# Loading the first head pair in halves, and a new written-out order, in a sparse-attention plus ELU-MLP kernel

## The chip, the cores and the metric

The kernel runs on one core of a Trainium2 chip. The metric is the device time of one execution in microseconds (us); lower is better. The program is bound to one core, so nothing is shared with another core by the program itself.

## The reference

```python
# q, k, v: (8, 8, 576, 64)  (batch, heads, positions, head size)
scores = q @ k.transpose(0, 1, 3, 2) / sqrt(64)
rel = pos[:, None] - pos[None, :]
mask_local   = (rel >= 0) & (rel < 32)                 # heads 0 to 3
mask_strided = (rel >= 0) & (pos % 32 equal for both)  # heads 4 to 7
attn = softmax(where(mask, scores, -1e9))
x = (attn @ v).transpose(0, 2, 1, 3).reshape(8 * 576, 8 * 64)   # 4608 tokens x 512
h = x @ w_in                                            # 512 -> 2048
g = where(h > 0, h, exp(min(h, 0)) - 1)                 # ELU
out = g @ w_out                                         # 2048 -> 512, float32
```

## The kernel before

All data is cast to bf16 on the way in; sums are kept in float32 in PSUM, whose eight banks of 512 columns are one tile `ps` that the program hands out by hand.

**Attention.** A sequence of 576 positions is cut into 8 residues of 72 rows each (for the strided heads, key and query of one residue meet only within it) or into six blocks of 96 (for the local heads). The heads of a batch come in four pairs: two strided (`s0`, `s1`) and two local (`l0`, `l1`), and each pair in two halves `u`. For batches 0 and 1 the rows of q and k are brought into columns by TensorE transposes (`transposes`, then `copy_T` out of PSUM); for later batches a DMA does it (`dma_T`). A pair then goes through `scores` (TensorE), `exp_s` (ScalarE), `mask` (VectorE), `pv` (TensorE: values and, for the softmax's sum, a matmul with ones), `log_sums` and `recip` (ScalarE: logarithm, and exponential of its negative), and `write_x` (VectorE), which puts the result into `xT`, the transposed input of the MLP.

**MLP.** The 4608 tokens are nine chunks of 512. The first product of a chunk is 16 steps of four matmuls over 512 columns (`l1`; in chunk 0 its four parts are split in two, first the two that need the strided heads alone, then the two that need the local heads). ELU is `exp_h` (ScalarE), `clamp` (VectorE or ScalarE) and `elu` (VectorE). The second product (`l2`) is four groups of 16 matmuls, then a copy out of PSUM and a store.

**Order.** Nothing is left to a scheduler: the string `ORDER` names every step, and each engine and each DMA queue takes its steps in that order. A token is a letter and its arguments: `T` transposes, `C`/`c` `copy_T` on ScalarE/VectorE, `S` scores, `e` exponential, `m` mask, `O` values, `n` logarithm, `r` reciprocal, `x` write to `xT`; `a`, `b` the two halves of a first-product step of chunk 0, `L` a whole one, `h`, `i`/`j`, `g` the ELU; `Z` a quarter of a second-product group, `o`/`q` its copy, `t` its store, `Y`/`y` the last group in pieces; `D` a load (`load`), `F` a fill of masks or ones, `V`, `W` copies of v, `X` a transposing DMA, `k`/`K` a cast of the staged q and k. In `S`, `O`, `T`, `a`, `L`, `Z` the last figures are PSUM banks. `w` is a run of matmuls on a tile of zeros (`warm`), whose result nobody reads; it fills TensorE's time in the first 20 us.

**The start.** q and k of the first strided pair (heads 4 and 5 of batch 0) are loaded ahead of the order by `load_stage`, each as one float32 transfer from SyncE's queue into `stage`, and cast by `cast`, one head at a time on ScalarE and VectorE. Everything else is loaded, and cast on the way, from GpSimd's queue, in the order of the `D` tokens: the second strided pair's q and k (`load_runs` of two heads), then v of the strided heads, k and q of the local heads, v of the local heads, and the weights in pieces of 512 columns (`wi1` holds steps 4 to 7 of the first product, `wi0` 0 to 3, `wi2` 8 to 11, `wi3` 12 to 15). One `load_runs` is a single transfer of all four heads.

Of the kernel before, what the change touches and what calls it, by code (L numbers as in the profile page):

```python
# [9 lines left out]
BF16 = mybir.dt.bfloat16  # L10
# [6 lines left out]
D = 64  # L17
# [28 lines left out]
i.0.7 a.0.11.7 g.0.1 h.0.3 b.0.0 g.0.7 h.0.5 T.1s1.q.1 b.0.6 h.0.0 i.0.2 a.0.8.3 c.1s1.q h.0.6 b.0.11  # L46
g.0.2 j.0.0 D.vs.1 a.0.13.1 i.0.3 b.0.8 h.0.11 g.0.0 a.0.12.5 j.0.5 g.0.3 b.0.13 i.0.6 a.0.14.0 h.0.13
b.0.12 g.0.6 D.vl.1 a.0.10.2 g.0.5 h.0.12 a.0.9.4 h.0.8 i.0.12 b.0.10 j.0.11 b.0.14 j.0.13 Z.0.0.0.6
g.0.11 h.0.10 D.vs.2 g.0.13 Z.0.2.0.7 h.0.14 g.0.12 j.0.14 Z.0.1.0.1 i.0.8 D.ks.2 i.0.10 Z.0.2.1.7
g.0.10 g.0.14 b.0.9 D.qs.2 T.1s0.q.5 g.0.8 h.0.9 T.1s1.k.2 a.0.15.0 c.1s0.q j.0.9 Z.0.1.1.1 c.1s1.k  # L50
# [20 lines left out]
L.2.2.6 W.3 h.2.7 i.2.7 L.2.11.5 D.vs.4 h.2.2 g.2.7 D.vl.3 L.2.3.4 h.2.11 j.2.2 i.2.11 S.3s0.0.01
S.3s0.1.23 L.2.6.7 g.2.2 e.3s0.0 D.qs.4 g.2.11 h.2.3 L.2.5.6 D.ks.4 e.3s0.1 m.3s0.0 i.2.3 h.2.6 D.ql.4
L.2.9.5 m.3s0.1 h.2.5 i.2.6 L.2.0.3 g.2.3 h.2.9 g.2.6 j.2.9 L.2.10.4 i.2.5 h.2.0 g.2.9 O.3s0.1.01 h.2.10
L.2.4.7 g.2.5 j.2.10 i.2.0 L.2.8.5 h.2.4 g.2.10 n.3s0.1 L.2.14.6 i.2.4 D.kl.4 g.2.0 h.2.8 L.2.1.4 g.2.4
# [638 lines left out]
```

## Time and profile before

| | us |
|---|---|
| median of 3 runs (lowest, highest) | 309.84 (309.32, 311.02) |
| the profiled execution, its own time | 310.17 |
| its span from first to last instruction | 308.5 |
| TensorE, busy | 300.1 (97% of the span) |
| ScalarE, busy | 231.1 (75%) |
| VectorE, busy | 224.9 (73%) |
| GpSimd, busy | 78.9 (26%) |

Instructions are named by the line of the kernel that issues them: L376 is a matmul on zeros, L382 a cast of staged q or k, L394 and L397 TensorE's transposes (strided, local), L405 to L409 the copies out of PSUM, L433 the scores, L440 their exponential, L447 and L453 the masks, L460 to L481 the values of batches 0 and 1 and their sums, L531 the logarithm, L536 the reciprocal, L561 the write to `xT`, L588 the first product, L622 the second, L596 to L616 the ELU. L231, L254, L265 and L269 are GpSimd's loads. The page counts a matmul as busy to its modelled end, which lies beyond the start of the next, so a busy TensorE does not say that no slot between two starts was lost.

### The profile page before, as it was taken

To read this page: it belongs to the slowest core of one execution; us is meant where nothing else is said; L and a number is where in the kernel's file an instruction comes from. 1 tells how busy PE (TensorE), PEld (TensorE's weight loads), DVE (VectorE), ACT (ScalarE), POOL (GpSimd) and SP (SyncE) were. 2 spreads that over 40 slices of the span, in tenths; PEclk is the share of its full clock that TensorE was granted. 3 is DMA by queue.
4 is the path that set the end of the run, shared out by engine and by line. 5 is a ranking of instruction groups with operands and counts; after the bars stand their busy time and mean duration, and the time that the engine had idled before them with its cause. 6 is when DMAs were issued, how large, how long until landed. Compare 5 with 4: busy or idle time off the path is not lost.

```text
span 308.5 us, 6465 instructions
## 1 busy us (share of the span) xinstructions
PE 300.1 (97%) x2452; PEld 154.0 (50%) x2452; DVE 224.9 (73%) x432; ACT 231.1 (75%) x413; POOL 78.9 (26%) x107
## 2 busy tenths in 40 slices
PE   8999999999999999999999999999999999999992
PEld 8864455445544454444544555454444544444452
DVE  6667969699679977996779879976688548984010
ACT  4888768689969898996998988888786577872120
POOL 8823345171029108530861250000000000000000
PEclk9999999999999999999999999999999999999999
DMA  8999999999909999999999199504110030100152
GB/s 165 192 208 205 207 194 176 144 216 156 203 9 167 160 225 116 163 187 158 193 187 125 17 145 189 108 24 130 56 34 0 2 102 0 36 1 0 36 162 77
DMA packets 106879, 37.61 MB, mean 122 GB/s; under 512 B 89024, under 2 KB 102048, under 8 KB 106848
## 3 DMA queue, kind: packets, MB, share of 16 engines
q0 software_dynamic: 69600, 19.43, 61.2%
q1 hardware_dynamic: 37088, 17.70, 30.3%
q8 instruction: 19, 0.31, 0.4%
q14 instruction: 12, 0.10, 0.1%
q10 hardware_dynamic: 160, 0.07, 0.1%
HBM read 39.47 MB, written 9.44 MB: 159 GB/s over the span
## 4 chain that ended last, share of the span: by engine, by line
PE 86%; DVE 4%; ACT 3%; DMA 3%; issue 1%; POOL 1%; POOLq 0%; DVEq 0%; ACTq 0%
PE ps L622 39%; PE ps L588 35%; PE ps L433 3%; DMA ql<-in_q_dram 3%; PE ps L503 2%; PE ps L496 2%; ACT he L596 1%; PE ps L652 1%; PE ps L376 1%; DVE he L605 1%; ACT he L603 1%; DVE g L616 1%; DVE g L614 1%; ACT e L440 1%; PE ps L397 1%
## 5 line engine op out<-in xcount | busy, mean ns | idle before, releaser
L622 PE MATMUL ps<-w_out_sb,g 128*128 128x512 bf16 x560 | 133.4, 379 | 0.3 <-DVE g L614 0.3
L588 PE MATMUL ps<-xT,w_in_sb 128*128 128x512 bf16 x576 | 132.4, 379 | 0.8 <-DVE g L616 0.4
L596 ACT ACTIVATE he<-ps 128x512 f32<-128x512 f32 x144 | 80.4, 595 | 27.8 <-PE ps L588 25.9
L588 PEld LDWEIGHTS <-w_in_sb 128*128 128x128 bf16 x576 | 54.5, 98 | 64.7 <-issue 2.8
L622 PEld LDWEIGHTS <-g 128*128 128x128 bf16 x560 | 51.1, 98 | 55.2 <-issue 0.4
L616 DVE TENSOR_TENSOR g<-he,ps 128x512 bf16<-128x512 bf16 x90 | 60.0, 681 | 1.7
L561 DVE TENSOR_TENSOR xT<-ps,ln 64x576 bf16<-64x576 f32 (+1 forms) x64 | 42.6, 677 | 18.3 <-ACT ln L536 17.8
L440 ACT ACTIVATE e<-ps 72x576 bf16<-72x576 f32 (+1 forms) x64 | 39.1, 646 | 10.8 <-PE ps L433 9.2
L614 DVE SCALAR_TENSOR_TENSOR g<-he,ps 128x512 bf16<-128x512 bf16 x54 | 36.4, 681 | 14.2 <-ACT he L603 14.0
L605 DVE TENSOR_SCALAR he<-he 128x512 bf16<-128x512 f32 x90 | 39.0, 442 | 8.2 <-ACT he L596 7.4
L531 ACT ACTIVATE ln<-ps 64x576 f32<-64x576 f32 (+1 forms) x64 | 36.3, 583 | 8.9 <-PE ps L503 3.8
L536 ACT ACTIVATE ln<-ln 64x576 f32<-64x576 f32 (+1 forms) x64 | 38.9, 621 | 1.4
L603 ACT ACTIVATE he<-he 128x512 bf16<-128x512 f32 x54 | 33.4, 628 | 1.3 <-DVE g L616 0.7
L628 DVE COPY osb<-ps 128x512 f32<-128x512 f32 x23 | 15.7, 685 | 11.6 <-PE ps L622 11.1
L244 POOL DMA_DIRECT2D kl<-in_k_dram x24 | 17.7, 744 | 21.9 <-DMA kTl<-kl 9.5
L237 POOL DMA_DIRECT2D ql<-in_q_dram x24 | 19.6, 822 | 7.7 <-DMA w_out_sb<-in_moe_w_out_dram 4.3
L453 DVE TENSOR_TENSOR pm<-e,mask_l 128x576 bf16<-128x576 bf16 x32 | 14.3, 456 | 7.6 <-ACT e L440 7.0
L447 DVE TENSOR_TENSOR pm<-e,mask_s 72x576 bf16<-72x576 bf16 x32 | 14.2, 447 | 4.6 <-ACT e L440 4.4
L628 ACT COPY osb<-ps 128x512 f32<-128x512 f32 x12 | 7.0, 586 | 13.5 <-PE ps L622 13.5
L376 PE MATMUL ps<-zero 128*128 128x128 bf16 x148 | 12.7, 251 | 1.4 <-DVE zero L293 1.1
L231 POOL DMA_DIRECT2D vs<-in_v_dram x7 | 4.7, 669 | 35.2 <-DVE he L605 18.5
L254 POOL DMA_DIRECT2D vl<-in_v_dram x8 | 9.7, 1213 | 15.6 <-PE ps L503 12.4
(87 smaller groups left out, 160.7 us busy)
## 6 DMA issues: line engine op xcount, KB each, us to landing
out_dram<-osb SPq DMA_DIRECT2D x32, 144.0 KB
vl<-in_v_dram POOLq DMA_DIRECT2D x8, 288.0 KB, 8.4
w_in_sb<-in_moe_w_in_dram POOLq DMA_DIRECT2D x4, 512.0 KB, 13.5
w_out_sb<-in_moe_w_out_dram POOLq DMA_DIRECT2D x4, 512.0 KB, 17.6
vs<-in_v_dram POOLq DMA_DIRECT2D x6, 320.0 KB, 7.0
ql<-in_q_dram POOLq DMA_DIRECT2D x24, 72.0 KB, 8.2
kl<-in_k_dram POOLq DMA_DIRECT2D x24, 72.0 KB, 7.7
ks<-in_k_dram POOLq DMA_DIRECT2D x5, 320.0 KB, 7.9
```

Of the source, the lines that this page charges most:

```text
L440: nc.scalar.activation(e[0:R], tiles.pop(("S", key, u))[0:R], ACT.Exp, scale=scale)
L531: nc.scalar.activation(t, s_ps, ACT.Ln)
L536: nc.scalar.activation(t, t, ACT.Exp, scale=-1.0)
L561: nc.vector.tensor_mul(dst, o_ps, rc)
L588: nc.tensor.matmul(tiles["h", ch, m], lhsT=w_in_sb[:, c, m * 128:(m + 1) * 128], rhs=xT[:, c, ch * CHUNK:(ch + 1) * CHUNK], start=(c == 2) ...
L596: nc.scalar.activation(e, tiles["h", i[0], i[1]], ACT.Exp)
L603: nc.scalar.activation(e1, e, ACT.Relu, bias=1.0, scale=-1.0)
L605: eng.tensor_scalar(e1, e, scalar1=1.0, scalar2=1.0, op0=ALU.min, op1=ALU.subtract)
L614: nc.vector.scalar_tensor_tensor(dst, e1, -1.0, h, op0=ALU.mult, op1=ALU.max)
L616: nc.vector.tensor_tensor(dst, e1, h, op=ALU.max)
L622: nc.tensor.matmul(ops, lhsT=g[ch % 2][:, m, kk * 128:(kk + 1) * 128], rhs=w_out_sb[:, m, :], start=(m == 0), stop=(m == MC - 1), skip_gro ...
L628: eng(o_sb, tiles.pop(("o", int(ch), int(kk))))
```

## The change

`load_stage` is gone. q and k of the first pair are each loaded in two halves of every run, 256 of its 512 elements each, as four transfers: q's two from SyncE's queue and k's two from ScalarE's queue, ahead of the activation table. `cast` takes a half of both heads instead of one head. `transposes` and `copy_T` take an optional part, and for the first pair do four of the eight blocks at a time. `load` takes an optional pair `y`, so that the order can load two heads of four; v of the strided heads and q and k of the local heads of batch 0 are loaded so, as six transfers in place of three. The tile of zeros has 512 columns instead of 128, and `warm` takes a list of widths. The whole of `ORDER` is new: the order of steps in all nine chunks, the banks, and which engine takes some of the copies and clamps. The computation is the same.

```diff
 ORDER = """
-w.7.46 D.vs.0 F.vp D.kl.0 F.v1 D.ql.0 k.q.1 K.q.0 D.vl.0 F.ms T.0s0.q.7 D.wi1.0 k.k.0 K.k.1 D.wi0.0
-C.0s0.q w.3.26 T.0s0.k.6 T.0s1.k.5 C.0s0.k D.wi2.0 C.0s1.k D.qs.1 w.3.12 S.0s0.0.67 T.0s1.q.4 e.0s0.0
-S.0s0.1.01 c.0s1.q e.0s0.1 w.5.7 S.0s1.0.23 D.wi3.0 S.0s1.1.45 m.0s0.1 m.0s0.0 F.mk e.0s1.1 w.3.12
...
-D.kl.1 m.0l0.0 w.7.11 a.0.5.6 r.0l1.1 m.0l0.1 a.0.7.3 n.0l1.0 x.0l1.1 O.0l0.1.21 r.0l1.0 O.0l0.0.05
-n.0l0.1 x.0l1.0 a.0.6.4 n.0l0.0 a.0.4.7 r.0l0.1 r.0l0.0 D.wo2.0 a.0.2.5 x.0l0.1 x.0l0.0 a.0.1.1 a.0.3.2
-b.0.7 b.0.4 h.0.7 b.0.1 h.0.4 D.ql.1 b.0.2 h.0.1 b.0.5 i.0.4 a.0.0.0 g.0.4 j.0.1 b.0.3 D.wo3.0 h.0.2
...
+w.7.512.512.512.512.512.512.512.512 D.ql.0.1 F.vp D.kl.0.1 F.v1 D.ql.0.0 k.q.0 F.ms D.vs.0.0 T.0s0.q.0.7
+D.kl.0.0 K.q.1 K.k.1 D.vs.0.1 K.k.0 C.0s0.q.0 w.0.512.512.512.512.512 T.0s0.k.0.6 D.vl.0 T.0s0.k.1.5
+T.0s0.q.1.4 c.0s0.k.0 T.0s1.k.7 c.0s0.k.1 c.0s1.k w.0.324 T.0s1.q.6 c.0s0.q.1 D.wi1.0 S.0s0.0.01 c.0s1.q
+S.0s0.1.23 e.0s0.0 w.5.185 S.0s1.0.45 D.qs.1 S.0s1.1.67 e.0s1.0 m.0s0.0 w.2.224.224 T.0l1.k.1 D.wi3.0
+e.0s1.1 m.0s1.0 w.0.499 T.0l0.q.0 C.0l1.k D.wi0.0 m.0s1.1 T.0l1.q.7 e.0s0.1 c.0l1.q w.4.155 O.0s0.0.16
+D.wi2.0 c.0l0.q n.0s0.0 w.4.314 S.0l1.1.45 S.0l1.0.23 m.0s0.1 F.mk r.0s0.0 T.0l0.k.7 O.0s0.1.60 e.0l1.1
+x.0s0.0 D.wo0.0 F.ml e.0l1.0 w.0.224.224.102 O.0s1.1.15 c.0l0.k n.0s0.1 D.wo1.0 w.4.247 O.0s1.0.43
+n.0s1.1 m.0l1.0 n.0s1.0 r.0s1.1 D.ql.1 w.2.512.512.108 S.0l0.0.23 x.0s1.1 e.0l0.0 V.0 w.7.512.331
+S.0l0.1.01 r.0s1.0 m.0l1.1 r.0s0.1 w.7.512 O.0l1.0.75 m.0l0.0 e.0l0.1 O.0l1.1.32 x.0s1.0 n.0l1.0 m.0l0.1
+w.2.224.224 O.0l0.0.10 n.0l1.1 x.0s0.1 r.0l1.0 w.1.142 O.0l0.1.54 r.0l1.1 x.0l1.0 D.ks.1 n.0l0.0
+w.4.224.224 a.0.5.6 x.0l1.1 n.0l0.1 a.0.7.7 r.0l0.0 a.0.4.0 r.0l0.1 x.0l0.0 a.0.6.4 D.kl.1 x.0l0.1
+T.1s1.q.3 b.0.5 c.1s1.q b.0.7 h.0.5 b.0.4 h.0.7 i.0.5 b.0.6 h.0.4 g.0.5 T.1s0.q.5 D.wo2.0 a.0.12.3
+C.1s0.q i.0.4 a.0.13.6 h.0.6 g.0.4 a.0.14.5 b.0.12 a.0.15.2 h.0.12 b.0.15 j.0.6 D.vs.1 a.0.2.1 j.0.12
+b.0.13 g.0.6 b.0.2 h.0.13 g.0.12 a.0.1.4 h.0.2 i.0.7 b.0.1 i.0.13 a.0.3.3 g.0.7 h.0.1 D.wo3.0 b.0.3
+i.0.2 b.0.14 h.0.3 g.0.2 a.0.0.7 j.0.1 b.0.0 a.0.11.1 g.0.1 h.0.0 a.0.10.0 h.0.14 D.vl.1 i.0.0 b.0.10
...
-    zero = consts.tile([128, 128], BF16, tag="zero", name="zero")
+    zero = consts.tile([128, CHUNK], BF16, tag="zero", name="zero")
...
-    def load(what, b):
+    def load(what, b, y=None):
         nm, b = what[:2], int(b)
+        if y is not None:
+            load_runs(nm, b, 2 * int(y), 2)
+            return
...
-    load_stage(0, q)
-    load_stage(1, k)
+    def half(t, i):
+        return t.rearrange("p (h f) -> p h f", h=2)[:, :, i * NS * D // 2:(i + 1) * NS * D // 2]
+
+    for eng, n, x in ((nc.sync, 0, q), (nc.scalar, 1, k)):
+        for i in range(2):
+            rows, in_ = runs(x, 0, HG, 2)
+            f = NS * D // 2
+            eng.dma_start(out=half(stage[0:rows, n * 4 * f:(n + 1) * 4 * f], i),
+                          in_=in_[:, :, i * f:(i + 1) * f])
     nc.scalar.preload_act_table_set("natural_log_exp_and_others")
     load_runs("qs", 0, 2, 2)
     load_runs("ks", 0, 2, 2)
...
-    def warm(bank, n):
-        for _ in range(int(n)):
-            nc.tensor.matmul(ps[:, int(bank), 384:512], lhsT=zero, rhs=zero, start=True, stop=True,
+    def warm(bank, *cols):
+        for n in cols:
+            nc.tensor.matmul(ps[:, int(bank), CHUNK - int(n):], lhsT=zero[:, 0:128], rhs=zero[:, 0:int(n)],
+                             start=True, stop=True, skip_group_check=True)
...
+    def cast(eng, nm, i):
+        n, f = "qk".index(nm), 2 * NS * D
+        eng(half(raw[nm + "s"][0:RS, 0:f], int(i)), half(stage[0:RS, n * f:(n + 1) * f], int(i)))
```

More of the change, by code (lines that the diff above doesn't have):

```diff
@@ L46 @@
[L46 to L50, printed above, removed]
@@ L71 @@
[L71 to L74, printed above, removed]
-h.2.14 i.2.8 r.3s0.1 O.3s0.0.23 i.2.14 L.2.12.7 g.2.8 n.3s0.0 X.qs.4 g.2.14 r.3s0.0 L.2.13.5 x.3s0.1
@@ L372, in local_cols, with transposes @@
         return t.rearrange("k (s b p) -> k b s p", s=NS, b=3)[:, i]
[L374 to L389 removed]
+    def warm(bank, *cols):
[5 more added lines that the diff above has]
+        eng(half(raw[nm + "s"][0:RS, 0:f], int(i)), half(stage[0:RS, n * f:(n + 1) * f], int(i)))
+    def transposes(key, nm, *a):
+        P, bank, part = Pair(key), int(a[-1]), a[:-1]
+        t = ps[:, bank, :].bitcast(BF16)[:, 0:S // (1 + len(part))]
+        tiles["T", key, nm, *part] = t
+        src = rawof(nm + P.c, P.b)[0:RS].rearrange("p (h f) -> p h f", h=HG)
+        if part:
+            for i in range(NS // 2):
+                x, sp = divmod(i, NS // 4)
+                c0 = (NS // 2 * int(part[0]) + 2 * sp) * D
+                nc.tensor.transpose(t[:, i * RS:(i + 1) * RS], src[:, P.head(x), c0:c0 + 2 * D],
+                                    identity[0:RS, 0:RS])
+            return
         for i in range(NS):
```

212 lines of the change are left out of this document (103 added, 109 removed).

## The prediction

> **What bounds the kernel now.** I read the page first, then busy time by windows, the chain of waits, and the timeline of the first 23 us.
>
> ```profile
> span 308.5 us, 6465 instructions
> PE 300.1 (97%) x2452; PEld 154.0 (50%) x2452; DVE 224.9 (73%) x432; ACT 231.1 (75%) x413; POOL 78.9 (26%) x107
> L622 PE MATMUL ps<-w_out_sb,g 128*128 128x512 bf16 x560 | 133.4, 379 | 0.3 <-DVE g L614 0.3
> 9.69:22.37 12.68, 12.19 (x266) 9.32 (x265) 9.06 (x22) 11.40 (x27) 6.25 (x9) 1.00 1.43 198
> 21.27:303.00 281.73, 280.39 (x2080) 136.74 (x2076) 210.59 (x385) 216.45 (x385) 64.25 (x82) 1.00 0.91 119
> 60.00:140.00 80.00, 78.88 (x617) 38.43 (x616) 69.07 (x127) 71.20 (x124) 31.88 (x41) 1.00 1.39 159
> 259.72 12.12 PE ps L588 x56
> ```
>
> The window rows give length, then busy time of PE, PEld, DVE, ACT, POOL, the granted clock, DMA share and GB/s. From 21.27 on PE is busy 280.39 of 281.73 us: it sets the time, and no other engine does. 56 wide matmuls take 12.12 us in the chain, 0.216 us each; the 379 ns of the page is 0.16 us more because a matmul counts to its modelled end, so waits shorter than that are not in the 1.34 us of idle. The change does not alter how many wide matmuls there are. So it can win only by starting this stream earlier, or in the waits inside it.
>
> The start is another matter. There PE is kept busy with zeros, so its share says nothing; one reads who starts when.
>
> ```profile
> 0.81 0.38 SPq L283 DMA_DIRECT2D g<-in_q_dram  x1
> 1.06 5.09 PE L376 MATMUL ps<-zero 128*128 128x128 bf16 x46 [1.06 <-DVE zero L293]
> 4.25 0.62 ACT L382 CAST qs<-g 72x512 bf16<-72x512 f32 x1 [2.16 <-DMA g<-in_q_dram]
> 4.59 0.39 DVE L382 CAST qs<-g 72x512 bf16<-72x512 f32 x1
> 5.55 0.62 ACT L382 CAST ks<-g 72x512 bf16<-72x512 f32 x1 [0.69 <-DMA g<-in_k_dram]
> 5.62 0.99 DVE L382 CAST ks<-g 72x512 bf16<-72x512 f32 x1
> 5.94 0.69 PE L394 MATMUL ps<-identity,qs 72*128 72x72 bf16 x8
> 6.44 1.78 PE L376 MATMUL ps<-zero 128*128 128x128 bf16 x26
> 8.05 0.68 PE L394 MATMUL ps<-identity,ks 72*128 72x72 bf16 x16
> 8.51 1.18 ACT L407 COPY kTs<-ps 128x576 bf16<-128x576 bf16 x2 [1.21 <-PE ps L394]
> 9.34 0.30 PE L433 MATMUL ps<-qTs,kTs 64*128 64x72 bf16 x8
> 9.69 1.25 ACT L440 ACTIVATE e<-ps 72x576 bf16<-72x576 f32 x2
> 13.80 0.62 ACT L409 COPY kTl<-ps 128x576 bf16<-128x576 bf16 x1
> 14.66 0.63 ACT L405 COPY qTl<-ps 128x576 bf16<-128x576 bf16 x1
> 21.27 6.22 PE L588 MATMUL ps<-xT,w_in_sb 128*128 128x512 bf16 x28
> 21.59 0.78 ACT L536 ACTIVATE ln<-ln 128x288 f32<-128x288 f32 x2
> 22.07 0.82 DVE L561 TENSOR_TENSOR xT<-ps,ln 128x288 bf16<-128x288 f32 x2 [1.06 <-ACT ln L536]
> 4.54 8.62 DMA ql<-in_q_dram
> ```
>
> Two things stand in it. The zeros overran: q was cast by 4.98 (4.59 + 0.39), but PE, strictly in order, was still in its 46 zeros until 5.94; k was cast by 6.61, but 26 more zeros ran until 8.05. That is 0.96 and 1.44 us in which the first pair waited for filler. Then from the first exponential at 9.69 to the last reciprocal at 22.37 (21.59 + 0.78) ACT is busy 11.40 of 12.68 us, while the chain of waits names the load of local q, 4.54 to 13.16. ACT's 1.28 us of idle is all that any earlier load can give back after 9.69; the rest is ACT's own work.
>
> **The change part by part.** *Halves and wide zeros.* The eight zeros of 512 columns cost 4 x 0.106 us each (46 of 128 took 4.88 us, 1.06 to 5.94), 3.4 us. With a longer memset of the zero tile ahead of them (0.1 us is my guess, and q's landing hides it) they end at 4.6. The first q half needs its transfer and one ACT cast: q landed whole at 4.25, and half of it beside half of k, the same bytes, at about the same time; 4.25 + 0.62 = 4.87, so four transposes run at 4.9 to 5.2 (0.49 us for eight, 5.94 to 6.44). Five wide zeros follow, 2.1 us at that speed: 7.2. ACT meanwhile casts k's second half, then its first, after the second has landed; all stage bytes had landed by 5.55, giving 5.55 + 2 x 0.62 = 6.8. So k's transposes start at about 7.1 against 8.05: 0.95 us.
>
> The trace bears on the split as follows: k's issue began 0.44 us after q's at 0.81, and k's cast could start 1.30 us after q's, so it was the moving of bytes that took the time. The Trainium skill has a rule that speaks against two queues: DMA: Bandwidth & Descriptors, "Issuing engines are not separate DMA queues", says that transfers from different engines share the same 16 DMA engines and that only issue time is saved. The trace agrees with it, and I count no earlier landing of the last half.
>
> On the clock, 46 matmuls at 0.106 us in a row, and the next 26 in 1.61 us (6.44 to 8.05, 0.062 each), show that speed nearly doubled in those 26. The skill's TensorE: Matmul & The Clock Gate, Part 1, puts the change after some 3.4 us of busy time, in a window that does not start with the kernel; the trace has it 5.4 us or more after the first matmul, so it differs from that figure here. By the rule the five zeros would take 1.1 us, and ACT's 6.8 would set the start, 0.3 us sooner.
>
> *To the first exponential.* Before: 8.05 to 9.69. After: k's eight and q's other four transposes, the eight of k and of q of the second pair (28 at 0.032, 16 having taken 0.52 us from 8.05 to the next start at 8.57) and 324 columns of zeros (0.14) end at 8.15. VectorE's two half copies run beside them and end by 7.95. Scores then start at 8.15, the exponential 0.35 later, as 9.34 to 9.69: 8.5 against 9.69, 1.2 us.
>
> *ACT from there.* The same 24 steps, but one copy of local q moves to VectorE: 11.40 - 0.63 = 10.77 us. VectorE has 3.6 us free in that window (9.06 of 12.68), so it hides there; uncovered it would cost 0.46. Idle: before 1.28; after, the second pair's scores wait for five copies in a row on VectorE, about 0.4 us after the first exponential ends, and some 0.5 us elsewhere: 0.9. Bounds are 0.3 and 2. The last reciprocal ends at 8.5 + 10.8 + 0.9 = 20.2, the last write to `xT` 0.5 us later (22.89 against 22.37): first `b` step at 20.7.
>
> *Loads.* Six transfers instead of three are three more issues on GpSimd.
>
> ```profile
> 3.92 0.64 POOL L231 DMA_DIRECT2D kl<-in_k_dram  x1
> 6.35 2.27 POOL L265 DMA_DIRECT2D w_in_sb<-in_moe_w_in_dram  x3
> 10.78 1.80 POOL L340 MEMSET ql<- 16x2048 bf16 x1
> 9.22 0.78 POOL L265 DMA_DIRECT2D w_in_sb<-in_moe_w_in_dram  x1
> DMA to landing us min/median/max: 10.6/13.5/17.1
> ql<-in_q_dram POOLq DMA_DIRECT2D x1, 320.0 KB, 8.6
> vs<-in_v_dram POOLq DMA_DIRECT2D x1, 320.0 KB, 5.4
> ```
>
> At 0.64 us each they hold GpSimd's queue for 1.9 us: the other loads, the mask fills, the memset behind them. The landing row is that of the four w_in pieces; the first, issued at 6.35, landed at 16.95, so 1.9 us less of 10.6 us of queueing is hidden. The price if not: 1.9 us on whatever waits. The masks, done on GpSimd by 10.78, would be by 12.7; VectorE reaches them, after the first pair's reciprocal, at about 13: hidden, barely. Batch 1's strided q and `wi3` now go ahead of `wi0` and `wi2`. At some 2.5 us a piece (16.95 for the first, 9.22 + 17.1 = 26.3 for the last, with three others between) they land at about 18.3, 20.8, 23.4 and 25.9. PE asks for batch 1's q at 20.4, `wi3` at 22.7, `wi0` at 25.3, `wi2` at 29.6: 1.9 us or more to spare, so no wait, but a start much sooner than mine would meet the loads.
>
> *The stream.* At 20.7 the new order has done four `a` steps, 8 wide matmuls, and one transposition of 8 (0.26); the old one's first `b` came after 14, at 21.27 + 10 x 0.216 = 23.43, the first four having run before 21.27. So 6 x 0.216 - 0.26 = 1.04 us more is left to do. The sum: 20.7 + 1.04 - 23.43 = -1.7 us. The re-ordering behind it, banks and engines anew, has the same 64 scores, 64 value steps, 268 whole steps of `L` and `Z`, and the same last six steps; copies and clamps move by one or two between ACT and VectorE. I take 0 for its waits. Bounds: all idle gone and as much again that the modelled ends hide, -2.7; on the other side as under the rivals, +4. I take 0 as the idle of 1.34 us is near it.
>
> The profiled execution took 310.17, 0.33 over the median of 309.84 and 1.7 over its span. So 308.5 for a profiled execution, **308.1 us** for the median.
>
> **The rivals.** *The start gives less.* ACT idles 2 us instead of 0.9 because one of the eight small loads is late or the clock stays slow past 8.5 us, so that scores, transposes and values cost double. The load of local q, 8.6 us from issue against 5.4 for v, shows that one load can lag. Gain 0.6, 309.2 us. Against it: all but the first steps have an exponential in hand on ACT.
>
> *The stream gives too.* If the new banks halve the hidden and seen waits, 2 us come on top: 306.1. For it: in the old order a bank is refilled as little as one `L` step, 0.86 us, after the value step that filled it; in the new one never under three.
>
> *Slower: the stream waits more.* Its place is 60 to 140 us, where ACT is busy 71.20 of 80 us.
>
> ```profile
> 99.06 1.09 ACT he L596 x2
> 100.19 1.02 DVE he L605 x2
> 101.74 0.68 DVE g L616
> 102.41 1.03 DVE xT L561 x2
> 103.67 0.68 DVE g L614
> ```
>
> Here the chain leaves PE and runs through ELU and an attention write. If the new order puts attention's logarithms ahead of the ELU that frees a bank, each such place costs PE about one ACT step, 0.54 us. It takes over from the gain at three such places and is slower by more than 0.5% from six; at seven, 3.8 us: 309.84 - 1.7 + 3.8 = 311.9. Against it: today's whole stream shows 1.34 us of idle.
>
> **How the numbers follow.** 0.5% is 1.55 us, about what a measurement of this kernel can tell from no change. Chances: the forecast (-0.9 to -2.7) 0.53, the start gives less 0.20, the stream gives too 0.14, slower 0.13. Faster by over 0.5%: three quarters of the forecast, 0.40, with 0.14: 0.54. Within: 0.13 and 0.20: 0.33. Slower by over 0.5%: 0.13. Range: 305.6 (a little past the stream's case) to 311.5 (into the slower case).
>
> **What would show it.** In the changed profile: k's transposes near 7.1 instead of 8.05, the first exponential near 8.5, ACT busy above 10.5 of some 11.7 us from there, the first product unbroken from about 19, its `b` steps at 20.7, PE idle after 21 us of 1 to 2 us, the same 5.5 us from 303 us, where the last matmul ends, to the end of the span at 308.5. I am wrong if PE waits for a load after 8 us, if the first exponential is past 9.3, or if PE's idle in 60 to 140 us is over 3 us.

## The result, and the profile after

| kernel | median, us | lowest to highest | executions |
|---|---|---|---|
| before | 309.83 | 309.32 to 311.02 | 4 |
| changed | 307.74 | 307.41 to 308.14 | 4 |

The ratio is 0.9898, with a 95% interval of 0.986 to 0.9936: faster by 1.0%, or 2.1 us. The profiled execution of the changed kernel took 308.06 us, its span 306.3 (before: 310.17 and 308.5). Executions of one and the same program differ here in one respect that some numbers below need: in some of them TensorE's granted clock falls to a half for 7 to 14 us within the first 26 us, and the mean clock beside the time tells which.

The timeline of the changed kernel's start; the columns are start, length, engine, line and operation, and in brackets the idle time before and what ended it.

```profile
0.81 0.93 ACTq L293 DMA_DIRECT2D g<-in_k_dram  x2
1.26 3.56 PE L382 MATMUL ps<-zero 128*128 128x512 bf16 x8 [1.26 <-DVE zero L299]
4.58 0.62 ACT L387 CAST qs<-g 72x512 bf16<-72x512 f32 x1 [1.53 <-DMA g<-in_q_dram]
5.39 1.25 PE L382 MATMUL ps<-zero 128*128 128x512 bf16 x5
6.12 1.14 ACT L387 CAST ks<-g 72x512 bf16<-72x512 f32 x2 [0.92 <-DMA g<-in_k_dram]
7.31 0.43 PE L398 MATMUL ps<-identity,ks 72*128 72x72 bf16 x8 [0.67 <-ACT ks L387]
8.81 0.65 ACT L457 ACTIVATE e<-ps 72x576 bf16<-72x576 f32 x1 [1.26 <-PE ps L450]
12.92 1.80 POOL L346 MEMSET ql<- 16x2048 bf16 x1
13.22 1.68 DVE L349 COPY mask_l<-mask 128x288 bf16<-128x288 bf16 x2
15.66 0.30 PE L450 MATMUL ps<-qTl,kTl 64*128 64x96 bf16 x6 [0.53 <-DVE kTl L426]
19.98 0.77 ACT L553 ACTIVATE ln<-ln 128x288 f32<-128x288 f32 x2
21.45 1.89 PE L605 MATMUL ps<-xT,w_in_sb 128*128 128x512 bf16 x8
```

k's transposes begin at 7.31 instead of 8.05, the first exponential at 8.81 instead of 9.69, the first `b` step at 21.45. The zeros hold nobody up any more: TensorE waits for q's cast (4.58 + 0.62) and k's cast, not they for it. But at 13.22 VectorE's two mask copies take 1.68 us beside a GpSimd memset (1.04 in the kernel before), and the second local half's scores wait for the copy behind them.

From the first exponential to the last reciprocal, and from the first `b` step to 303 us, by windows:

```profile
8.81:20.75 11.94, 10.94 (x210) 7.17 (x212) 10.21 (x24) 10.63 (x25) 9.32 (x13) 1.00 1.42 196
21.45:303.00 281.55, 276.25 (x2027) 136.35 (x2063) 210.82 (x383) 214.63 (x382) 64.89 (x82) 1.00 0.91 119
```

ACT is busy 10.63 of 11.94 us. PE's 276.25 us are understated: 40 of the 2339 matmuls have no record in this trace, as its page shows:

```profile
PE 294.3 (96%) x2299; PEld 146.8 (48%) x2339; DVE 227.3 (74%) x435; ACT 228.6 (75%) x412; POOL 81.7 (27%) x110
```

The changed kernel once more, on another chip, has all of them; a row of its windows:

```profile
60.00:140.00 80.00, 79.50 (x636) 39.03 (x635) 69.76 (x128) 70.17 (x124) 27.18 (x35) 1.00 1.38 163
```

To split the gain, three points are read that both orders pass after the same work: the weight load of chunk 1's first product, the end of the last matmul, and the end of the span. First the kernel before (timeline: that weight load and the last store's issue):

```profile
55.29 0.55 PEld L588 LDWEIGHTS <-w_in_sb 128*128 128x128 bf16 x3
...
304.53 1.11 SPq L640 DMA_DIRECT2D out_dram<-osb  x2
```

and the last matmuls in its chain of waits:

```profile
299.46 3.55 PE ps L652 x48
```

Then the changed one, in the same two views:

```profile
54.41 0.53 PEld L605 LDWEIGHTS <-w_in_sb 128*128 128x128 bf16 x3
...
303.00 1.11 SPq L657 DMA_DIRECT2D out_dram<-osb  x2
```

```profile
297.94 3.55 PE ps L669 x48
```

Up to chunk 1 the gain is 55.29 - 54.41 = 0.88 us. From there to the last matmul's end (303.01 and 301.49) it is 247.72 - 247.08 = 0.64. From that end to the end of the span it is 5.5 - 4.8, about 0.6. Sum 2.1 us, the difference of the two spans with their rounding.

### The profile page after: what moved, and what is told of

Its sections match the earlier page's. It is cut to its first block, busy times and chain, and to the rows that moved or that the text cites. A ratio compares the mean times of both kernels' runs of the same rounds, so it can differ in the third digit from the quotient of the medians.

```text
span 306.3 us, 6219 instructions
## 1 busy us (share of the span) xinstructions
PE 294.3 (96%) x2299; PEld 146.8 (48%) x2339; DVE 227.3 (74%) x435; ACT 228.6 (75%) x412; POOL 81.7 (27%) x110
## 4 chain that ended last, share of the span: by engine, by line
PE 86%; DVE 6%; ACT 2%; issue 2%; DMA 2%; ACTq 0%; DVEq 0%
PE ps L639 39%; PE ps L605 36%; PE ps L450 3%; DVE g L633 2%; PE ps L520 2%; PE ps L513 2%; DVE he L622 2%; DMA g<-in_k_dram 2%; PE ps L669 1%; ACT he L613 1%; DVE mask_l L349 1%; DVE xT L578 1%; PE ps L493 0%; ACT e L457 0%; PE ps L408 0%
## 5 line engine op out<-in xcount | busy, mean ns | idle before, releaser
L639 PE MATMUL ps<-w_out_sb,g 128*128 128x512 bf16 x538 | 129.6, 379 | 2.0 <-issue 0.6
L605 PE MATMUL ps<-xT,w_in_sb 128*128 128x512 bf16 x559 | 129.4, 379 | 1.6 <-issue 0.3
L633 DVE TENSOR_TENSOR g<-he,ps 128x512 bf16<-128x512 bf16 x92 | 62.0, 684 | 1.9
L457 ACT ACTIVATE e<-ps 72x576 bf16<-72x576 f32 (+1 forms) x64 | 39.1, 647 | 13.4 <-PE ps L450 11.7
L622 DVE TENSOR_SCALAR he<-he 128x512 bf16<-128x512 f32 x92 | 40.1, 445 | 7.7 <-ACT he L613 7.0
L631 DVE SCALAR_TENSOR_TENSOR g<-he,ps 128x512 bf16<-128x512 bf16 x52 | 34.8, 682 | 7.2 <-ACT he L620 6.9
L620 ACT ACTIVATE he<-he 128x512 bf16<-128x512 f32 x52 | 32.5, 630 | 1.6 <-DVE g L633 1.1
L513 PEld LDWEIGHTS <-vsp 72*128 72x128 bf16 x192 | 9.1, 98 | 5.4 <-DVE pm L464 0.3
```

The source lines that it names most:

```text
L457: nc.scalar.activation(e[0:R], tiles.pop(("S", key, u))[0:R], ACT.Exp, scale=scale)
L605: nc.tensor.matmul(tiles["h", ch, m], lhsT=w_in_sb[:, c, m * 128:(m + 1) * 128], rhs=xT[:, c, ch * CHUNK:(ch + 1) * CHUNK], start=(c == 2) ...
L620: nc.scalar.activation(e1, e, ACT.Relu, bias=1.0, scale=-1.0)
L622: eng.tensor_scalar(e1, e, scalar1=1.0, scalar2=1.0, op0=ALU.min, op1=ALU.subtract)
L631: nc.vector.scalar_tensor_tensor(dst, e1, -1.0, h, op0=ALU.mult, op1=ALU.max)
L633: nc.vector.tensor_tensor(dst, e1, h, op=ALU.max)
```

## The experiments

All changes are against the changed kernel, but for the last run, which is the kernel before. The first eight ran on one chip, where the kernel before had a median of 310.43 beside the first four and of 311.33 beside the next four; the last four ran on a third chip, where it had 310.07 and where the changed kernel itself was not run.

### The changed kernel again, and its start with the old stream

No edit in the first. Expected:

> The changed kernel once more, on the chip of the next three, as the measure for them. Both theories: 307.4 to 308.2 us, first b step of chunk 0 (first matmul of the unbroken first product after batch 1's transpose) at 21.4, the masks copied on VectorE in 1.7 us from 13.2.

Measured: 307.4 us (306.81 to 307.81, 6 executions), ratio 0.989 (0.9855 to 0.9925). Chunk 1 begins at 54.16, the last group's weight loads at 296.92.

The second keeps the new start up to the last write of batch 0 and then goes on in the old order, with the weights loaded in the old order too:

```diff
-S.0s0.1.23 e.0s0.0 w.5.185 S.0s1.0.45 D.qs.1 ... D.wi3.0 ... D.wi0.0 ... D.wi2.0
+S.0s0.1.23 e.0s0.0 w.5.185 S.0s1.0.45 D.wi0.0 ... D.wi2.0 ... D.qs.1 ... D.wi3.0
...
-w.4.224.224 a.0.5.6 x.0l1.1 n.0l0.1 a.0.7.7 ...
+w.4.224.224 a.0.5.6 x.0l1.1 n.0l0.1 a.0.7.3 r.0l0.0 a.0.4.7 ... (the old order from here on)
```

> The changed kernel's start up to the last write of batch 0, then the old order of everything after it, with the weights loaded in the old order. Theory A (the start gives about 1 us, the stream about half of that, and the end of the last store the rest): first b step at 21.3 to 21.6, the last group of the second product begins about 0.5 to 0.8 us before that of the old kernel (299.3), so 308.8 to 309.3 us. Theory B (all of the gain lies in the start): the last group begins at 297.8 and the time is that of the changed kernel, 307.4 to 308.2. Theory C (the start gives nothing, the new stream all): the old kernel's time, 309.5 to 310.

Measured: 308.7 us (308.31 to 309.35), ratio 0.9927 (0.9892 to 0.9962). Its timeline near 30 us:

```profile
29.73 1.19 POOL L251 DMA_DIRECT2D vl<-in_v_dram  x1 [1.98 <-DVE g L626]
29.99 1.15 DVE L617 TENSOR_SCALAR he<-he 128x512 bf16<-128x512 f32 x1
31.91 1.46 PE L600 MATMUL ps<-xT,w_in_sb 128*128 128x512 bf16 x6 [0.50 <-DVE g L628]
...
55.26 0.53 PEld L600 LDWEIGHTS <-w_in_sb 128*128 128x128 bf16 x3
```

The time is about theory A's, the way to it is not. By the starts of the matmuls in the two traces, the first product is 0.66 us ahead of the kernel before up to the one at 31.03, and no longer ahead from 31.91 on; chunk 1 begins at 55.26, where the kernel before has 55.29. All that the start had won was lost in one place. A clamp of 0.42 us took 1.15 beside a GpSimd load issue of 1.19, the ELU product behind it came late, and TensorE, which needed its bank, stood still for 0.50. So the new order of chunk 0 does its share: in the old one, in this profile, the earlier start is worth nothing at chunk 1. That the profile is still shorter than that of the kernel before comes from behind chunk 1: 1.0 us in the stream (246.76 us to the last matmul's end at 302.02, against 247.72), and 0.6 at the very end, as in the changed kernel. In the medians the clock comes on top: its ten executions have a mean of 0.997 or more, while five of the fifteen of the kernel before beside it had 0.984 to 0.986 and 312 to 313.1 us.

### The masks

One line of theory: VectorE's mask copies wait out the memset. In the first kernel the memset stands behind the loads of the start; in the second the masks are filled and copied before 7 us as well.

```diff
-w.4.224.224 a.0.5.6 ... a.0.6.4 D.kl.1 x.0l0.1
+w.4.224.224 a.0.5.6 ... a.0.6.4 D.kl.1 F.mq x.0l0.1
...
+        elif what == "mq":
             nc.gpsimd.memset(odd["ql"][64:RP], 0.0)
```

> GpSimd's memset of 16x2048 moved behind the loads of batch 1. Theory A (the memset beside the mask copies on VectorE slows them, and they are what the local scores wait for): copies of the masks in 1.0 to 1.1 us instead of 1.68, the second local pair's scores 0.5 to 0.6 us earlier than 15.66, first b step 0.4 to 0.6 earlier, time 0.3 to 0.6 less than the changed kernel. Rival (another cause slows the copies, such as landing loads): copies still 1.5 to 1.7, no change.

Measured: 306.98 us (306.38 to 307.31), ratio 0.988 (0.9831 to 0.9928). Its timeline:

```profile
13.31 0.38 DVE L350 COPY mask_l<-mask 128x288 bf16<-128x288 bf16 x2
30.27 1.19 POOL L256 DMA_DIRECT2D vl<-in_v_dram  x1 [1.97 <-DMA w_out_sb<-in_moe_w_out_dram]
30.71 0.98 DVE L623 TENSOR_SCALAR he<-he 128x512 bf16<-128x512 f32 x1
36.50 0.68 DVE L634 TENSOR_TENSOR g<-he,ps 128x512 bf16<-128x512 bf16 x1
37.23 1.02 PE L640 MATMUL ps<-w_out_sb,g 128*128 128x512 bf16 x4 [0.28 <-DVE g L634]
```

and the same two VectorE steps, clamp and ELU product, in the changed kernel's repeat:

```profile
31.32 0.43 DVE L622 TENSOR_SCALAR he<-he 128x512 bf16<-128x512 f32 x1
36.45 0.68 DVE L633 TENSOR_TENSOR g<-he,ps 128x512 bf16<-128x512 bf16 x1
```

The copies take 0.38 us instead of 1.68, and the first `b` step comes 0.6 sooner (20.94 against 21.56 in the repeat above). Yet chunk 1 begins at 54.18, as in that repeat (54.16). The rows say where most of it went: the clamp at 30.71 took 0.98 us instead of 0.43, beside a load issue of 1.19 as above, and the ELU product that TensorE needs at 37.23 ended at 37.18, where the repeat's ended at 37.13. VectorE has little room there to catch up: in both kernels it is busy 3.57 and 3.69 of the 4 us in 28 to 32 and 32 to 36. Behind that wait TensorE is 0.17 us ahead of the repeat (37.23 against 37.40), and at its next transposes level with it (38.29 against 38.26), for which the traces name no cause. The 0.6 us were won and given back. The median is 0.4 us below the repeat's all the same, from a stream that is 0.4 us shorter behind chunk 1 (246.3 against 246.7), less than one program varies by there, as the last run shows.

```diff
-w.7.512.512.512.512.512.512.512.512 D.ql.0.1 F.vp
+w.7.512.512.512.512.512.512.512.512 F.mk D.ql.0.1 F.vp
-D.kl.0.0 K.q.1 K.k.1
+D.kl.0.0 K.q.1 F.ml K.k.1
...
```

> The mask fill done at the very start: GpSimd's two selections ahead of the local loads, VectorE's copies while it waits for k, the memset behind batch 1's loads. Theory A (masks hold up the start): second local pair's scores near 14.0 instead of 15.66, ScalarE's idle of 0.87 us there gone, first b step 0.9 to 1.3 us earlier, 306.6 to 307.3. Rival (ScalarE is full anyway, or a load then sets the pace, since each lands up to 0.7 us later): first b step less than 0.4 earlier.

Measured: 307.26 us (306.95 to 307.38), ratio 0.9889 (0.9842 to 0.9937). The second local half's scores came at 15.16, not at 14.0:

```profile
13.31 0.75 DVE L427 COPY kTl<-ps 128x576 bf16<-128x576 bf16 x1
14.57 0.65 PE L383 MATMUL ps<-zero 128*128 128x512 bf16 x3
```

The copy that they need is done at 14.06, but TensorE goes through values and sums until 14.5 and then through three zero matmuls that stand in the order ahead of the scores. Filler that was sized for the slower start is the next limit. Taking it out was not tried. The first `b` step comes at 20.83, 0.7 us sooner than in the repeat and between what the two theories say, and chunk 1 at 53.76, 0.4 sooner: here half of the gain gets there. The medians, 307.26 and 307.4, do not tell the two kernels apart.

### k's halves, their queue, and whole runs

```diff
-... K.q.1 K.k.1 D.vs.0.1 K.k.0 ...
+... K.q.1 K.k.0 D.vs.0.1 K.k.1 ...
```

> The changed kernel, with the casts of k's two halves in the other order: the half whose transposes come first is cast first (0.57 us a half; in the changed kernel both casts take 6.12 to 7.26 and k's first transpose follows at 7.31). Theory A (the start is held from 13 us on by the mask copies behind the GpSimd fill, not by q and k): k's first transpose comes 0.4 to 0.6 us earlier (6.7 to 6.9), the first score 0.2 to 0.5 earlier, and nothing of it reaches the first score of the second local pair (15.66 in the changed kernel) or the first second-product (21.3): both within 0.2, time within 0.3 of 307.4. Theory B (what I predicted: the first exponential sets the start, everything behind it moves with it): the first second-product 0.3 to 0.5 earlier, time 0.2 to 0.5 less.

Measured: 307.58 us (307.05 to 307.91), ratio 0.9873 (0.9813 to 0.9934).

```profile
6.62 0.64 PE L398 MATMUL ps<-identity,ks 72*128 72x72 bf16 x8
13.06 2.00 DVE L349 COPY mask_l<-mask 128x288 bf16<-128x288 bf16 x2
15.83 0.30 PE L450 MATMUL ps<-qTl,kTl 64*128 64x96 bf16 x6 [0.91 <-DVE kTl L426]
```

k's transposes come 0.7 sooner and the first scores 0.2 (8.25), and none of it passes the masks: the second local half's scores are at 15.83 against 15.66. What I had predicted, that all behind the first exponential moves with it, is wrong; theory A holds.

```diff
-    for eng, n, x in ((nc.sync, 0, q), (nc.scalar, 1, k)):
+    for eng, n, x in ((nc.sync, 0, q), (nc.sync, 1, k)):
```

> The changed kernel, with all four halves of the first pair's q and k issued from SyncE's queue, none from ScalarE's. Theory A (the two queues bring k sooner, as predicted): the four issues follow one another at 0.46 us, k's second half is issued at about 2.2 instead of 1.27 and lands up to 0.9 later (6.9 instead of 6.1); k's first transpose at 8.1, the first score 0.8 later, the first second-product 0.4 to 0.8 later, time +0.4 to +0.8. Theory B (both queues feed the same 16 engines, so that bytes and not queues bind): k's last half lands within 0.3 of 6.1, k's first transpose within 0.3 of 7.31, time within 0.3 of 307.4.

Measured: 312.95 us (312.3 to 314.93, 10 executions, mean clock 0.972 to 0.978 in all), ratio 1.006 (1.0023 to 1.0096). Both theories missed the time by far. Timeline and windows:

```profile
1.73 0.94 SPq L293 DMA_DIRECT2D g<-in_k_dram  x2
7.20 1.14 ACT L387 CAST ks<-g 72x512 bf16<-72x512 f32 x2 [3.17 <-DMA g<-in_k_dram]
8.39 0.43 PE L398 MATMUL ps<-identity,ks 72*128 72x72 bf16 x8 [1.60 <-ACT ks L387]
```

```profile
8.00:10.00 2.00, 1.55 (x37) 1.33 (x38) 1.19 (x5) 0.65 (x3) 1.58 (x4) 0.91 1.22 198
10.00:14.00 4.00, 3.94 (x76) 2.65 (x75) 1.79 (x5) 2.99 (x5) 3.74 (x6) 0.50 1.79 181
22.00:24.00 2.00, 2.00 (x28) 1.28 (x27) 0.95 (x3) 1.16 (x3) 0.51 (x1) 0.68 1.27 214
```

k is issued 0.92 us later (1.73 against 0.81) and cast 1.08 later. So far the Trainium skill has it right: DMA: Bandwidth & Descriptors, "Issuing engines are not separate DMA queues", says that a second issuing engine saves issue time only, and issue time is what was lost here. But TensorE, out of zeros, stood still for 1.60 us, and the granted clock, the third number from the end of a window's row, then reads 0.50. A clock of 0.91 over 8 to 10 us and of 0.68 over 22 to 24 puts the half speed from 9.6 to 23.3. The first `b` step came at 26.8, 5.3 us late.

```diff
-    for eng, n, x in ((nc.sync, 0, q), (nc.scalar, 1, k)):
+    for eng, n, x in ((nc.sync, 0, q), (nc.sync, 1, k)):
...
-... w.0.512.512.512.512.512 T.0s0.k.0.6 ...
+... w.0.512.512.512.512.512.512.512.512.512.512.512.512 T.0s0.k.0.6 ...
```

> The kernel with all four halves on SyncE's queue again (312.95 us, granted clock 0.50 from 9.63 to 23.28), with seven more 512-column zero matmuls where TensorE waited 1.5 us for k, from 6.8 to 8.3. Theory A (most of the 5.5 us that one queue cost is the clock, which falls to a half because TensorE stood still before k's transposes): no stretch of granted clock 0.50, mean clock 0.995 or more in nearly all executions, k's transposes still at 8.2 to 8.5, the first second-product at 22.0 to 22.6, time 307.9 to 308.6. Theory B (the late k and what queues behind it cost the 5.5 us): time stays above 311.

Measured, on the third chip: four executions at 307.84, 307.97, 308.18 and 309.16 us with a mean clock of 0.998 to 1.000, and six at 313.65 to 314.81 with 0.975 to 0.978. The median of all, 313.67, says little. In the four the time is theory A's, 0.3 to 0.7 us above the changed kernel's medians on the other two chips. The other six are some 6 us longer in the same program, at a mean clock that is 0.022 lower, which over 308 us is 13.6 us at half speed. So that is the price of the clock in the main; when k landed in the four, no trace shows. The profiled execution was one of the six, and its gap was not filled:

```profile
9.37 0.43 PE L398 MATMUL ps<-identity,ks 72*128 72x72 bf16 x8 [1.70 <-ACT ks L387]
```

k's cast began at 8.18, 1 us later still, and TensorE stood 1.70 us at the end of its twelve zeros. So the experiment shows what the fall costs, not that a filled gap rules it out. That six of ten fell here and ten of ten without the filler may be the filler or the chip.

```diff
-        for i in range(2):
-            eng.dma_start(out=half(stage[0:rows, ...], i), in_=in_[:, :, i * f:(i + 1) * f])
+        eng.dma_start(out=stage[0:rows, ...], in_=in_)
```

> The changed kernel, with q and k of the first pair loaded whole (2 KB runs, one DMA each: q from SyncE's queue, k from ScalarE's) and not in halves; the casts stay in halves. Theory A (the halves let q's transposes start sooner, which is hidden, and k, which sets the start, gains nothing from them): q's first cast 0.3 to 0.8 later than 4.58, k landed at 5.6 to 6.3, k's first transpose within 0.3 of 7.31, time within 0.3 of 307.4. Theory B (the halves are what brought k forward, as 1 KB packets and two issues for each tensor keep the engines fuller): k landed and its first transpose 0.5 to 0.9 later (7.8 to 8.2), the first second-product 0.4 to 0.8 later, time +0.4 to +0.8.

Measured: 309.03 us (307.84 to 309.59, mean clock 0.995 or more), ratio 0.9905 (0.9874 to 0.9937).

```profile
5.54 0.62 ACT L386 CAST qs<-g 72x512 bf16<-72x512 f32 x1 [2.99 <-DMA g<-in_q_dram]
6.06 1.13 ACT L386 CAST ks<-g 72x512 bf16<-72x512 f32 x2
6.21 0.42 PE L397 MATMUL ps<-identity,qs 72*128 72x72 bf16 x4 [1.35 <-ACT qs L386]
6.44 2.33 PE L381 MATMUL ps<-zero 128*128 128x512 bf16 x5
8.56 0.69 PE L397 MATMUL ps<-identity,ks 72*128 72x72 bf16 x8
```

The size is theory B's and more, its reason is not: k is cast as early as before (6.06), but q 0.96 later, so the five zeros behind q's transposes start 1.05 later, and k's transposes wait for them. The clock has a part in it too: the zeros take 2.33 us instead of 1.25 and k's eight transposes 0.69 instead of 0.43, that is, TensorE still runs at half speed. The trace's record of the granted clock begins with its first rise, here at 10.70 us, in the changed kernel at 4.66; the mean clock leaves out the time ahead of it. So halving k's runs gained nothing that this run shows, and halving q's did, by way of TensorE's strict order. How much of it is the late rise, one profile does not say; the ten executions spread from 307.84 to 309.59.

### Local q and k by head pairs

```diff
-... D.ql.0.1 F.vp D.kl.0.1 F.v1 D.ql.0.0 k.q.0 F.ms D.vs.0.0 T.0s0.q.0.7
-D.kl.0.0 K.q.1 K.k.1 D.vs.0.1 K.k.0 ...
+... D.vs.0 F.vp D.kl.0 F.v1 D.ql.0 k.q.0 F.ms T.0s0.q.0.7
+K.q.1 K.k.1 K.k.0 ...
```

> The changed kernel, with strided v, local q and k of batch 0 as three whole loads in the order of the kernel before (v, k, q), not six loads by head pairs; all else, its order on TensorE too, unchanged. Theory A (the head pairs and their order are what let the local transposes stand early): the local q, k land 10.2 to 12.0 instead of 8.1 to 11.8 and the local pair's first transposes, which stand before the second exponential's work, wait: the first local score 1 to 2 us later, the first second-product 0.8 to 2 us later (22.1 to 23.3), time +0.6 to +1.8. Theory B (the loads have room, what holds the start is ScalarE and the masks): the first second-product within 0.3 of 21.3, time within 0.3 of 307.4.

Measured: 311.51 us (308.63 to 312.35), ratio 1.0007 (0.9973 to 1.004). One execution, the profiled one, has a mean clock of 0.997 and 308.63 us, within theory A; the nine others have 0.982 to 0.988 and 310.25 to 312.35.

```profile
12.07 0.71 PE L408 MATMUL ps<-identity,ql 72*64 72x72 bf16 x32 [0.71 <-DMA ql<-in_q_dram]
```

TensorE waits 0.71 us for local q, and the first `b` step is at 22.12, 0.6 late. Taking the head pairs and their order away takes back the whole gain: of 4.1 us over the repeat's median on the same chip, 1.2 are there without a fall of the clock.

### Narrow zeros

```diff
-w.7.512.512.512.512.512.512.512.512 ...
+w.7.128.128.128. ... (each width cut into pieces of 128 or less, all through the start)
```

> The changed kernel with each zero matmul over 128 columns cut into pieces of 128 or less, as many columns as before in the same places (70 matmuls more). Theory A (the width changes nothing that the path sees; the columns keep the clock, not the instructions): k's first transpose and the first second-product within 0.3 of 7.31 and 21.3, time within 0.4 of 307.4, no execution with a mean clock under 0.99. Theory B (narrow zeros with a weight load each leave TensorE's array idle between them, and the clock falls in some executions as it did in the kernel before): some executions 2 to 3 us longer at a mean clock of 0.98 to 0.99, the others within 0.4 of 307.4.

Measured, on the third chip: 308.07 us (307.16 to 310.96), ratio 0.9936 (0.9906 to 0.9966); the first `b` step is at 21.57. One execution of ten (310.96) has a mean clock of 0.988, the others 0.996 or more. The width changes nothing on the path; whether it bears on the clock, one case in ten does not settle. The interval overlaps that of the changed kernel.

### Three edits together

The memset later, the masks early and k's first half first, as shown above.

> The changed kernel with three edits together: the memset of 16 x 2048 on GpSimd moved behind the start's loads, the masks' copies ahead of it, and k's first half cast first. Theory A (between 20 and 45 us the loads, at 205 GB/s without a gap, set when the second batch's q and k land, so what the start gains is given back there): the first second-product 20.3 to 20.7, but the second batch's first local-free transposes still at 36.5 to 37.2, the last group within 0.4 of 296.6, time 306.8 to 307.4. Theory B (the start's gain of 0.7 to 1.0 reaches the end): time 306.3 to 306.7.

Measured, on the third chip: 307.7 us (306.68 to 313.47), ratio 0.9922 (0.9896 to 0.9949). Two executions were far longer, 311.37 us at a mean clock of 0.981 and 313.47 at 0.999; no trace shows the second's cause. In the profile, at 307.37 us, the first `b` step is at 20.89 (neither theory's 20.3 to 20.7) and chunk 1 at 53.89. The time is nearer to theory A's, but the reason that I gave for it, the loads, does not show: the trace lists no wait of TensorE for a load between 20.5 and 54.5 us. The clamp beside the load issue takes 0.79 us here, and the lead over the repeat is 0.67 us at the `b` step, 0.46 at the wait for the ELU product (36.94 against 37.40) and 0.27 at chunk 1. No version here beats the changed kernel by more than the intervals hold; the lowest median is that of the later memset, 306.98.

### The kernel before, once more

> The kernel before once more, for its profile on this chip, where 13 of 25 of its executions took 311.3 to 313.3 us at a mean granted clock of 0.985 to 0.989 and the others 309.6 to 311.1 at 0.993 to 0.999. If this execution is one of the long ones, the theory of the clock expects one stretch of about 10 us at clock 0.50 inside the first 35 us, begun by a standstill of TensorE of over 1 us in the 3.4 us before it, and a stream of the same length as in the first profile behind it. If it is one of the short ones, no such stretch, and the stream's waits between 60 and 110 us and the last store's landing show how far these vary.

Measured: 312.16 us, mean clock 0.985. Timeline, windows, and the last matmuls in the chain of waits:

```profile
6.95 0.42 PE L394 MATMUL ps<-identity,ks 72*128 72x72 bf16 x8
8.94 1.25 ACT L440 ACTIVATE e<-ps 72x576 bf16<-72x576 f32 x2 [0.27 <-PE ps L433]
13.47 0.71 PE L397 MATMUL ps<-identity,ql 72*64 72x72 bf16 x32 [1.19 <-DMA ql<-in_q_dram]
...
58.20 0.53 PEld L588 LDWEIGHTS <-w_in_sb 128*128 128x128 bf16 x3
```

```profile
14.00:16.00 2.00, 1.92 (x38) 1.65 (x31) 1.50 (x5) 1.31 (x3) 1.11 (x2) 0.67 1.27 206
20.00:22.00 2.00, 2.00 (x28) 1.45 (x29) 0.37 (x1) 1.02 (x3) 0.75 (x1) 0.62 1.24 206
```

```profile
301.42 3.55 PE ps L652 x48
```

This is the kernel before when the clock falls. TensorE stood 1.19 us waiting for local q, and from 14.7 to 21.5, 6.8 us and not about 10, the clock was a half; chunk 1 began at 58.20 instead of 55.29. From there to the last matmul's end (304.97) it took 246.77 us, 0.95 less than in the first profile: the old stream varies by that much by itself. The end of the span (310.4) again lay 5.4 us behind the last matmul.

What came ahead of the standstill matters as much. The clock had risen sooner, at 4.45 us by the trace's record instead of 6.78, so the zeros went faster: k's transposes began at 6.95 (8.05 in the first profile, 7.31 in the changed kernel) and the first exponential at 8.94 (9.69 and 8.81). The same filler that overran in the first profile ran out here before local q had landed, at 13.4 (4.53 + 8.9). So filler that is counted in matmuls is too long at one speed and too short at the other.

## Why the prediction was right, and where its steps were not

The time was right: 307.74 against 308.1 and, for the profiled execution, 308.06 against 308.5. Its parts were not all.

**Zeros and first pair.** Forecast: zeros done at 4.6, q's transposes at 4.9, five zeros to 7.2 at the slow speed, k's at 7.1. Measured 4.82, 5.25, 6.64, 7.31. Two errors of opposite sign. The clock went up at 4.66 us, before the five zeros, which took 1.25 us, not 2.1. And k's bytes landed at 6.12, not 5.55, so ACT idled 0.92 us before its cast. I took it that halves beside each other bring the same bytes at the same time; they came 0.6 later. What I had priced as the zeros' overrun is also not a property of the kernel before alone: in its second profile, where the clock rises sooner, k's transposes come 0.36 us ahead of the changed kernel's and the first exponential only 0.13 behind.

**First exponential and ACT.** 8.81 against 8.5. ACT's work was 10.63 us against 10.77, its idle 1.31 against 0.9, so the last reciprocal ended at 20.75 and not at 20.2.

**The masks, the step that failed.** I had the mask fills and the memset done late by three load issues and called it "hidden, barely". The delay was sized well (the memset at 12.92 against 10.78 before, 2.1 us for my 1.9), its effect was not: the copies do not just come after GpSimd's fill, they are held up by the memset beside them. The trace of before had shown it, 1.04 us for the two copies beside the memset at 10.78, and I had not read it so:

```profile
11.71 1.04 DVE L343 COPY mask_l<-mask 128x288 bf16<-128x288 bf16 x2
```

The Trainium skill has the rule, in SBUF — State Buffer, "Who interferes with whom": VectorE's copies and tensor_scalar operations can use a pair of ports that GpSimd has as well, the pair is locked for a whole instruction, and the other engine blocks. The traces agree: 0.38 us alone, 1.68, to 14.90, beside a memset that ends at 14.72; and a clamp of 0.43 alone, 0.98 and 1.15 beside a load issue. Not every such clamp is held up: in the trace of the later memset, 8 of the 29 clamps that overlap GpSimd's work take over 0.5 us, and none of the other 63. The memset cost 0.6 us at the first `b` step, as the later memset shows.

**The start's worth.** Forecast 1.7 us, measured 0.88 at chunk 1. The first `b` step was at 21.45 and not at 20.7; with the 1.04 us more work left, 23.43 - 21.45 - 1.04 = 0.94, which is what arrived. The rest was to be had in part at most: with the masks out of the way the `b` step came 0.6 to 0.7 us sooner, and chunk 1 not at all (the later memset), 0.3 (the three edits) or 0.4 sooner (the masks early). I had warned that a much earlier start would meet the loads; it met VectorE's ELU and a clamp beside a load issue.

**Loads.** Forecast 18.3, 20.8, 23.4 and 25.9; landed at 18.75, 22.17, 24.06 and 26.6, by 0.5 to 1.4 us too late. The least to spare was 1.3 us (`wi3`, asked for at 23.43) for my 1.9, and TensorE waited for none, so this step held.

**The stream.** Forecast no change in its waits; measured 0.64 less from chunk 1 to the last matmul. The old kernel's second profile is 0.95 shorter there than its first, and the old order on the new start (246.76) is as long as the new order's repeat (246.69), so no effect of the new order beyond chunk 1 is shown; 60 to 140 us has 0.5 us of idle in the changed kernel's repeat. The slower rival, seven places with late ELU, did not come.

**The end.** I said the same 5.5 us behind the last matmul; it is 4.8. The stores are issued as before; behind the last issue it is 2.8 us (305.64 to 308.5) in the kernel before and 2.2 (304.11 to 306.3) in the changed one. Both profiles of the kernel before have the longer end. The old order on the new start has the shorter one (4.9 us) and the new order with whole runs of q and k a longer one again (5.4), so the order is not what makes it; no run tells the cause.

**The clock, which no step held.** I treated it as a matter of the first 8 us. In three profiles TensorE stood still for over a microsecond in the first 15 us, after the clock had risen, and in all three the clock then fell back to a half. Beside the four experiments on k's and local q's loads that ran on the second chip, 13 of 25 executions of the kernel before had a mean clock of 0.985 to 0.989 and took 311.3 to 313.3 us; all ten of the changed kernel had 0.998 or more. With the three whole loads put back, nine of ten fell again. The two profiles of the result, at 310.17 and 308.06 us, have no fall, so it is no part of their difference. But on the second chip, where the changed kernel is 3 to 4 us below the kernel before, part of the gain, by the mean clocks, is not an earlier start but a fall of the clock that no longer comes; in the one profile of the kernel before that has it, a wait for local q went ahead of it. On where the limit lies: 1.60, 1.70 and 1.19 us of standstill came before a fall; 0.67 (the changed kernel), 0.71 (whole loads, its profiled execution) and 0.91 (k's first half first) before none, and neither did 0.55 and 0.71 close together (the repeat); between 0.91 and 1.19 it is open. The 1.35 us with whole runs of q and k came ahead of the clock's first rise, and that rise was the latest of all the profiles: 10.70 us, against 4.1 to 7.2. The Trainium skill's TensorE: Matmul & The Clock Gate, Part 1, gives a window of 3.41 us that runs by itself; the half-speed stretches here, 6.8 and 13.7 us, are two and four of them. Its section "Why this matters for your kernels" allows gaps of about 3 us; here a fall came behind one of 1.19 us, and the measurement decides.

Of the three signs that I had named for being wrong (a wait for a load after 8 us, a first exponential past 9.3, over 3 us of idle in 60 to 140 us) none came; the mask copies were on no list.

So the sum was right because a start worth half of the forecast was joined by 0.6 us at the end that I had not seen and 0.6 in a stream that varies by more. That is luck. What held is the mechanism in outline: TensorE's stream starts sooner, no load holds it up, and its waits grow no longer.

## What to carry to other kernels

When a change moves work on GpSimd's queue, ask which VectorE copies or clamps will then run beside it, not only who waits for its results: here a memset and load issues stretched some of them to between two and four times their length. Filler for TensorE should be judged at both of its speeds, by the longest standstill that it leaves near the start, and by what stands behind it once the real work comes sooner. Before an earlier start is counted as gain, find the engine that is nearly full behind it; here VectorE, at 3.6 of 4 us from 28 to 36, with a clamp held up in it, took back between a third (three edits together) and three quarters (the later memset) of what the masks had given.

## What the runs showed of the hardware that I had not expected

A standstill of 1.2 to 1.7 us in the first 15 us was followed by TensorE at a granted clock of 0.50 for 6.8 us (the kernel before) and 13.7 us (one queue), which went with a chunk 1 that began 2.9 us later and with times 5 to 6 us longer. The clock's first rise came between 4.1 and 10.7 us in starts that differ little. One program fell in six of ten executions and not in four, so a single profile need not show it; the mean clock beside each time does. A GpSimd memset of 1.80 us stretched two VectorE copies from 0.38 to 1.68 us, and a load issue of 1.19 us on GpSimd stretched a clamp from 0.43 to 0.98 and 1.15.
